# Attention weights of heads 0 to 7 transposed on TensorE instead of VectorE and DMA, with the feed-forward weights decoded earlier

## The chip, the cores and the metric

The kernel runs on one core of a Trainium2 chip. The metric is the device time of one execution in microseconds (us). Three runs of the kernel before took 759.37, 759.25 and 757.38 us; the median is 759.25 us. Engines are named as in the profile: PE (TensorE matmuls), PEld (its weight loads), DVE (VectorE), ACT (ScalarE), POOL (GpSimd), SP (the queue that issues the DMAs).

## The reference, cut to what matters

Two layers over 8 batches of 576 tokens; all numbers are float32.

```python
# attention: 64 heads (8 batches x 8 heads), 576 tokens, head dimension 64
scores = q @ k.T / 8;  cum = cumsum(max(s, 0))
scores = where(causal, -1e9, scores + min(-(cum[i] - cum[j]), 0))
attn   = softmax(scores);  x = attn @ v          # heads side by side: 576 x 512 per batch
# feed-forward with a gate over the sequence
h = gelu(x @ w_in); u, v = h[:, :512], h[:, 512:]
v = layernorm(v) * g_ln
out = x + (u * (w_sg @ v + b_sg)) @ w_out
```

## The kernel before, in words

Heads run in pairs; batch b is heads 8b to 8b+7, and its feed-forward part starts when its fourth pair is done, beside the attention of batch b+1. Thus heads 0 to 7 have no feed-forward work beside them. What fills that stage otherwise is the preparation of the feed-forward weights: `w_in` and `w_out` arrive as 64-bit floats (tile `wraw`, 16 and 8 pieces) and are decoded by integer operations (tiles `wbits`, `wm`) into a high and a low part (`wi`, `wo`); `w_sg` (`wst`, `ws`) is only split in two.

One head is five strips of scores, 64, 192, 320, 448 and 576 columns wide (1600 in all). Heads 0 to 11 (`NQ = 12`) use plain float32 matmuls on a prepared tile `kf`; later heads load `raw` and split it into `k` and `low`. Each strip goes through `softmax` (line 912): PE writes scores into PSUM (`sc`, the widest strip `sx`), DVE adds the mask and finds the row extreme `mn`, ACT takes the exponential in place and sums it (`sum`), and DVE's STREAM_TRANSPOSE turns it into the SBUF tile `ex`. That instruction transposes 32x32 blocks, so quarters of 32 partitions of a 64x64 block end up in the wrong place.

`shuffle` (line 970) mends this once per pair: two DMAs copy quarters of `ex` to a side tile `pt`, two DMAs move other quarters inside `ex`, and then ACT and POOL each copy 32x1600 numbers from `pt` back to `ex`. Only then can `pv` (line 990), PE's product of the weights with `v` into the tiles `xx`, start. It is recorded as one group, and DVE then scales `xx` into `xr` by the row `rb`, which has come from `sum` by way of two small DMAs (`rd`, `rb`). `ex` has room for two pairs. PSUM holds six one-bank tiles (tag `m`, shared by `sc`, `xx` and the feed-forward tiles `vm`, `um`, `sm`, `om`) and one two-bank tile for `sx`.

No instruction is written in its final place. Everything is recorded with a key (a position in units of heads: `POS` at line 58, `place` and `spread` at lines 1169 to 1190), a table `SHIFT` (line 74) moves kinds of operations by some units, and `plan` (line 549) lists all operations engine by engine, choosing the next by key among those that are ready by its own estimates. The order of each engine, SP's included, is then fixed in the program. Because all instructions are emitted by one helper, the profile gives them all line L528; they are told apart by their tiles.

Of the kernel before, what the change touches and what calls it, by code (L numbers as in the profile page):

```python
# [49 lines left out]
NQ = 12  # L50
U2 = 5
# [6 lines left out]
POS = dict(load=-2.0, split=-1.0, sc=(0, 0, 0, 0), sh=0.0, pv=1.9, wv=(0.1, 7.5),  # L58
           wu=(7.0, 10.0), ws=(9.0, 11.0), wo=(11.0, 14.0), f0=2.0, f1=9.6)
# [34 lines left out]
    "act copy k 128x576 raw": (-8.09, 6.2, -1.34, 101.2, 0.56),
    "act copy k 64x576 raw": (5.62, 5.49, 15.59, 99.03, 9.86),
    "act copy low 64x576 raw": (12.89, 12.94, 12.94, 0.06, -5.16),
    "act copy vt 64x512 vm": (-8.41, -2.47, -2.5, -5.05, -5.92),
    "act copy wi 128x256 wbits": (-0.48, 5.93, -3.16, 3.66, -17.79),
    "act copy wo 128x256 wbits": (-14.55, 8.67, 10.51, -13.27, 9.97),
    "act copy wr 128x576 wst": (0, -2.7, -2.97, -2.88, -0.18),  # L100
    "act copy wr 1x576 wst": (-12.69, -14.66, -18.24, -15.87, -18.2),
    "act copy ws 128x576 wst": (-13.38, -11.05, -21.02, -1.37, -1.37),
# [6 lines left out]
    "dve memset low 2x1152 -": (2.18, 1.59, -4.4, -13.47, 5.93),  # L109
    "dve memset maska 128x320 -": (0.83, 0.03, 3.82, 1.89, 0.62),  # L110
    "dve memset maskb 128x576 -": (-0.22, 0.2, 0.2, -0.22, -0.22),
    "dve memset sum 128x1 -": (-5.69, -7.9, -7.65, -6.26, -6.98),
    "dve memset sum 128x52 -": (-11.23, 7.01, 0.55, 0.74, 0.74),
    "dve memset vnr 33x512 -": (2.86, -3.96, 1.53, -17.46, -2.87),
# [3 lines left out]
    "dve reciprocal sum 128x10 sum": (14.09, 0.44, 0.44, 35.34, 6.22),  # L118
# [32 lines left out]
    "dve transpose rb 128x32 sum": (0.03, 0.03, 0.03, 0, -0.11),  # L151
# [1122 lines left out]
```

## Time and profile before

| | us |
|---|---|
| median of three runs | 759.25 |
| the profiled execution, its own time | 762.57 |
| its span from first to last instruction | 760.9 |
| PE busy in the span | 692.3 |
| DVE, ACT, POOL busy | 577.5, 536.8, 485.7 |

The page gives busy time by engine and, in 40 slices of 19 us each, the busy tenths of each engine and the TensorE clock that was granted, in tenths of its full speed. Other views of the same trace name, for each engine, whom it waited for and how long, list instructions in order of time, and sum the busy time of every engine in a stretch. A count such as x68 is the number of instructions; a plain float32 matmul shows as two instructions on PE.

### The profile page before, as it was taken

The numbers are of one execution on the slowest core, as the hardware profiler recorded it, in microseconds if no ns is written. First come the engines' busy times: TensorE is split into PE (matmuls) and PEld (weight loads), VectorE is DVE, ScalarE is ACT, GpSimd is POOL, SyncE is SP. The second block draws the span as 40 slices with busy tenths as digits, with TensorE's granted clock in tenths as the row PEclk, the third lists the DMA queues.
The fourth block names the chain that finished last, engine by engine and source line by source line (L and its number), as shares of the span: only waits on it lengthen the run. The fifth ranks groups of instructions, "written<-read, shape, count | busy, mean of one in ns | idle before, by whom it ended". The sixth has DMA issues, their size and how long they took to land.

```text
span 760.9 us, 16999 instructions
## 1 busy us (share of the span) xinstructions
PE 692.3 (91%) x5858; PEld 620.5 (82%) x5858; DVE 577.5 (76%) x1657; ACT 536.8 (71%) x1290; POOL 485.7 (64%) x634
## 2 busy tenths in 40 slices
PE   7567587799998999989998999989998999999998
PEld 5355376699887989889887989889987989899998
DVE  8775869987688776978688877978687877973752
ACT  4654578787779786878688886978688876952431
POOL 6242678878666866667756865767756865753631
PEclk9777888889999999999999999999999999999999
DMA  7564875525364363445444464435454464423101
GB/s 222 140 171 125 220 173 147 144 81 149 102 170 132 110 171 111 114 127 160 120 125 132 119 161 120 121 111 163 117 127 128 127 155 133 107 79 85 54 9 62
DMA packets 64974, 97.47 MB, mean 128 GB/s; under 512 B 19972, under 2 KB 44676, under 8 KB 64888
## 3 DMA queue, kind: packets, MB, share of 16 engines
q1 hardware_dynamic: 64888, 96.39, 46.9%
q8 instruction: 46, 0.75, 0.4%
q14 instruction: 40, 0.33, 0.2%
HBM read 56.72 MB, written 10.26 MB: 88 GB/s over the span
## 4 chain that ended last, share of the span: by engine, by line
PE 48%; DVE 12%; DMA 10%; ACT 9%; POOL 6%; issue 3%; SPq 0%; POOLq 0%; DVEq 0%; ACTq 0%
PE sm L528 10%; PE vm L528 9%; PE om L528 9%; PE xx L528 8%; PE um L528 7%; DMA raw<-in_kq 4%; PE sc L528 3%; DVE ex L528 3%; ACT sc L528 2%; DMA pt<-ex 2%; PE sx L528 2%; ACT k L528 2%; DVE sc L528 2%; DMA out_t<-ot 2%; DVE u L528 1%
## 5 line engine op out<-in xcount | busy, mean ns | idle before, releaser
L528 ACT ACTIVATE sc<-sc,mn 64x64 f32<-64x64 f32 (+3 forms) x256 | 112.4, 439 | 42.1 <-DVE mn L528 39.2
L528 PE MATMUL sm<-ws,vn 128*128 128x288 f32 x768 | 130.3, 307 | 0.4 <-DVE ex L528 0.2
L528 PE MATMUL um<-xs,wi 128*128 128x288 f32 x768 | 119.7, 304 | 8.0 <-DVE ex L528 5.0
L528 PE MATMUL om<-gt,wo 128*128 128x288 f32 x768 | 119.7, 298 | 2.6 <-POOL gt L528 2.2
L528 DVE STREAM_TRANSPOSE ex<-sc 64x64 f32<-64x64 f32 (+3 forms) x256 | 107.0, 430 | 17.2 <-ACT sc L528 16.0
L528 PEld LDWEIGHTS um<-xs,wi 128*128 128x128 f32 x768 | 110.0, 194 | 10.3 <-DVE ex L528 5.2
L528 PE MATMUL xx<-ex,v 64*64 64x128 f32 (+4 forms) x2176 | 100.3, 334 | 18.1 <-ACT ex L528 13.8
L528 PEld LDWEIGHTS xx<-ex,v 64*64 64x64 f32 x2176 | 87.2, 146 | 35.5 <-ACT ex L528 16.5
L528 PEld LDWEIGHTS sm<-ws,vn 128*128 128x128 f32 x768 | 113.5, 196 | 2.6 <-DVE ex L528 1.2
L528 PEld LDWEIGHTS om<-gt,wo 128*128 128x128 f32 x768 | 107.7, 188 | 6.4 <-POOL gt L528 3.2
L528 ACT CAST k<-raw 128x576 fp32r<-128x576 f32 x156 | 104.8, 672 | 10.8 <-DMA raw<-in_kq 5.7
L528 PE MATMUL vm<-wi,xs 128*128 128x512 f32 (+1 forms) x416 | 110.7, 399 | 0.6 <-POOL xs L528 0.4
L528 PEld LDWEIGHTS vm<-wi,xs 128*128 128x128 f32 (+1 forms) x416 | 74.1, 184 | 17.0 <-POOL xs L528 2.3
L528 POOL TENSOR_TENSOR k<-raw,k 64x576 fp32r<-64x576 f32 x52 | 74.0, 1423 | 9.2 <-ACT k L528 6.9
L528 POOL TENSOR_TENSOR gt<-u,gt 128x288 fp32r<-128x288 f32 x64 | 50.8, 806 | 43.6 <-ACT gt L528 43.2
L528 DVE CUSTOM_DVE_ANT_0 sc<-sc,maska 128x192 f32<-128x192 f32 (+2 forms) x192 | 66.8, 355 | 15.4 <-PE sc L528 14.2
L528 POOL TENSOR_TENSOR low<-raw,k 64x576 fp32r<-64x576 f32 x52 | 73.9, 1422 | 4.4 <-DMA wst<-in_w_sgt 1.9
L528 DVE SCALAR_TENSOR_TENSOR u<-u,um 128x288 f32<-128x288 f32 x128 | 55.7, 441 | 27.6 <-ACT u L528 21.7
L528 POOL TENSOR_SCALAR ex<-pt 32x1600 f32<-32x1600 f32 x32 | 48.9, 1529 | 39.7 <-DMA ex<-ex 30.9
L528 PE MATMUL sc<-k 128*128 128x320 f32 (+1 forms) x208 | 60.3, 300 | 6.9 <-DVE vnr L528 4.2
L528 DVE TENSOR_TENSOR xr<-xx,rb 128x320 f32<-128x320 f32 x64 | 27.0, 447 | 50.1 <-PE xx L528 50.1
L528 ACT CAST gt<-u 128x288 fp32r<-128x288 f32 x64 | 25.8, 429 | 54.0 <-DVE u L528 42.7
(101 smaller groups left out, 1424.0 us busy)
## 6 DMA issues: line engine op xcount, KB each, us to landing
v<-in_vp SPq DMA_DIRECT2D x32, 576.0 KB
raw<-in_kq SPq DMA_DIRECT2D x52, 288.0 KB
pt<-ex SPq DMA_DIRECT2D x64, 200.0 KB
ex<-ex SPq DMA_DIRECT2D x64, 200.0 KB
rb<-rd SPq DMA_DIRECT2D x64, 160.0 KB
out_t<-ot SPq DMA_DIRECT2D x64, 144.0 KB
wraw<-in_w_in SPq DMA_DIRECT2D x16, 256.0 KB
kf<-in_kf SPq DMA_DIRECT2D x11, 292.5 KB
```

Source lines behind the costliest of these rows:

```text
L528: real[i] = [getattr(op["eng"].real, name)(*[f(a) for a in args], **{k: f(v) for k, v in kw.items()}).ins for args, kw in calls]
```

## The change

For heads below `NE = 8`, ACT writes the exponential not in place but into the side tile `pt` (each strip has its own columns, `EO`). PE then transposes it in pieces of 64x64: a matmul with the piece as the stationary operand and a 64x64 identity as the moving one, whose result goes back into the same PSUM tile. ACT copies the strip from PSUM to `ex`. There are 49 such matmuls for a head (1 + 2 x (3 + 5 + 7 + 9)), recorded per strip as one group called `turn`. DVE's transposes of these heads and the whole `shuffle` of the first four pairs are gone, and `pv` of these pairs has an earlier key (0.9 instead of 1.9). The identity lies in the last 64 columns of `wo` until those are decoded. The keys of the weight preparation are moved forward (`w_in` over heads 0 to 10 instead of 0 to 17, `w_out` from 7.5 instead of 11), and all of `SHIFT` is new, so every engine's order is planned again; the planner also has a cost for `turn` and for PE after a pause.

```diff
+NE = 8
+EO = [0, 64, 256, 576, 1024]
...
-POS = dict(load=-2.0, split=-1.0, sc=(0, 0, 0, 0), sh=0.0, pv=1.9, wv=(0.1, 7.5),
-           wu=(7.0, 10.0), ws=(9.0, 11.0), wo=(11.0, 14.0), f0=2.0, f1=9.6)
+POS = dict(load=-2.0, split=-1.0, sc=(0, 0, 0, 0), sh=0.0, pv=1.9, pe=0.9, wv=(0.1, 4.0),
+           wu=(3.5, 6.0), ws=(6.0, 8.0), wo=(7.5, 9.5), f0=2.0, f1=9.6)
...
-    "dve transpose ex 128x576 sx": (-13.44, -12.28, 343.35, 317.33, 0),
+    "dve transpose ex 128x576 sx": (-8.08, 20.99, 161.81, 299.85, -1.96),
...
+    eye = wo[:, NC - 1, 1, DM - 64:DM]
+    ident = eye.bitcast(F32)
+    nc.vector.memset(ident, 0.0)
...
         c = 5 * (h % 2) + it
-        nc.scalar.activation(out=o, in_=o, func=AF.Exp, bias=mn, scale=-1.0, accum_out=sums[h // 2 % 2][0:r, c:c + 1])
         n = w // 64
-        nc.vector.transpose(out=xt_[0:r].pattern(base(h) + 32 * cell(h % 2, it, 0), (32, n), (RG, 2), (1, 32)), in_=o)
+        e = o if h >= NE else pt_[0:r, EO[it]:EO[it] + w]
+        nc.scalar.activation(out=e, in_=o, func=AF.Exp, bias=mn, scale=-1.0, accum_out=sums[h // 2 % 2][0:r, c:c + 1])
+        x = xt_[0:r].pattern(base(h) + 32 * cell(h % 2, it, 0), (32, n), (RG, 2), (1, 32))
+        if h >= NE:
+            nc.vector.transpose(out=x, in_=o)
+            return
+        calls = []
+        for j in range(n):
+            for g in range(r // 64):
+                rows, cs = slice(64 * g, 64 * g + 64), slice(c0 + 64 * j, c0 + 64 * j + 64)
+                calls.append(((pst[rows, cs], e[rows, 64 * j:64 * j + 64], ident[rows]), dict(start=True, stop=True)))
+        nc.group(calls, "turn")
+        nc.scalar.copy(out=x, in_=o)
...
         if h % 2:
-            place(h + POS["sh"], shuffle, h)
-            place(h + POS["pv"], pv, h)
+            if h >= NE:
+                place(h + POS["sh"], shuffle, h)
+            place(h + POS["pv" if h >= NE else "pe"], pv, h)
```

On PE, around the first group `xx` (the weights of heads 0 and 1 times `v`), the order before is this. `sc<-kf` and `sx<-kf` are score matmuls.

```order
L528 MATMUL sc<-kf 128x320
L528 MATMUL sc<-kf 128x192
L528 MATMUL sc<-kf 128x448
L528 MATMUL sc<-kf 128x64
L528 MATMUL sx<-kf 128x256
L528 MATMUL sx<-kf 128x320
L528 MATMUL xx<-ex,v 64x320 x2
...
L528 MATMUL xx<-ex,v 64x2x32 x8
L528 MATMUL sx<-kf 128x256
L528 MATMUL sc<-kf 128x320
```

The same place now, where `sc<-wo,pt` and `sx<-wo,pt` are the transposing matmuls (`wo` holds the identity):

```order
L546 MATMUL sc<-wo,pt 64x64 x20
L546 MATMUL sx<-wo,pt 64x64 x18
L546 MATMUL sc<-kf 128x448
L546 MATMUL sc<-kf 128x64
L546 MATMUL sc<-wo,pt 64x64 x11
L546 MATMUL sx<-kf 128x256
L546 MATMUL sx<-kf 128x320
L546 MATMUL xx<-ex,v 64x320 x2
...
L546 MATMUL xx<-ex,v 64x2x32 x8
L546 MATMUL sc<-wo,pt 64x64 x20
L546 MATMUL sx<-wo,pt 64x64 x18
```

Before, nothing but scores stands ahead of the group and behind it; now transposes of later heads stand between the scores and directly behind the group.

On SP, from the request of `kf` for a later head to the small transfers for the first pair (`rd`, `rb`), before:

```order
L528 DMA kf<-in_kf 65x1152
L528 DMA pt<-ex 32x1600 x2
L528 DMA kf<-cf 1x16x36
L528 DMA rd<-rb 128x32
L528 DMA kf<-in_kf 65x1152
L528 DMA ex<-ex 32x1600 x2
L528 DMA rb<-rd 64x4x160 x2
```

And now:

```order
L546 DMA kf<-cf 1x16x36
L546 DMA wraw<-in_w_in 128x512 x2
L546 DMA rd<-rb 128x32
L546 DMA kf<-in_kf 65x1152
L546 DMA rb<-rd 64x4x160 x2
```

The four shuffle transfers of the pair are gone, and two pieces of `w_in` stand ahead of `rd`.

On DVE, the decoding of `w_out` (`wbits<-wraw,wbits`) stood before among the steps of batch 0's feed-forward part (`vt`, `vm`, `bs`, `u`), in the rows that lead up to the sixth pair's `xr`:

```order
L528 SCALAR_TENSOR_TENSOR wbits<-wraw,wbits 128x256
L528 SCALAR_TENSOR_TENSOR vt<-vm,bs,g_b 128x512
L528 STREAM_TRANSPOSE ex<-sc 64x2x32
L528 SCALAR_TENSOR_TENSOR wbits<-wraw,wbits 128x256
L528 SCALAR_TENSOR_TENSOR vm<-vt,vm 128x512
L528 SCALAR_TENSOR_TENSOR wbits<-wraw,wbits 128x256
L528 BN_STATS bs<-vm 128x6
L528 SCALAR_TENSOR_TENSOR wbits<-wraw,wbits 128x256
```

Now the last larger run of it stands behind the fourth pair's `xr`, among the softmax steps of the next heads:

```order
L546 STREAM_TRANSPOSE ex<-sx 128x9x2x32
L546 STREAM_TRANSPOSE ex<-sc 128x3x2x32
L546 SCALAR_TENSOR_TENSOR wbits<-wraw,wbits 128x256
L546 STREAM_TRANSPOSE ex<-sc 64x2x32
L546 TENSOR_SCALAR wbits<-wbits 128x256
L546 SCALAR_TENSOR_TENSOR wbits<-wraw,wbits 128x256 x4
L546 ISA sc,mn<-sc,maska 128x320
```

Of the 16 instructions of this kind, 7 now stand ahead of the fourth pair's `xr`, 7 between it and the fifth's, and 2 behind that.

## Rows read from the trace of the kernel before

**Rows 1.** From the page: span, PE busy, and PE's granted clock in 40 slices

```profile
span 760.9 us, 16999 instructions
...
PE 692.3 (91%) x5858; PEld 620.5 (82%) x5858; DVE 577.5 (76%) x1657; ACT 536.8 (71%) x1290; POOL 485.7 (64%) x634
...
PEclk9777888889999999999999999999999999999999
```

**Rows 2.** Four stretches: busy us of each engine (instructions), clock, DMA share, GB/s

```profile
0.00:101.00 101.00, 67.91 (x436) 50.50 (x437) 71.89 (x231) 53.28 (x150) 46.14 (x57) 0.81 0.69 176
101.00:180.00 79.00, 67.38 (x543) 59.95 (x546) 70.33 (x191) 63.22 (x150) 66.02 (x85) 0.89 0.51 138
180.00:696.00 516.00, 495.46 (x4458) 451.09 (x4459) 401.71 (x1168) 399.15 (x946) 346.39 (x442) 0.98 0.47 128
696.00:761.00 65.00, 61.59 (x428) 58.99 (x427) 33.55 (x69) 21.17 (x44) 27.11 (x52) 1.00 0.13 41
```

**Rows 3.** PE's waits from 0 to 101 us: total, times, longest

```profile
PE xx L528 <- ACT ex L528: 12.3, 3, 5.5
PE sx L528 <- DVE ex L528: 8.0, 4, 3.2
PE sc L528 <- DMA kf<-cf: 4.8, 2, 4.5
PE xx L528 <- DVE ex L528: 4.3, 1, 4.3
```

**Rows 4.** The first pair's shuffle in order of time: start, us, what, idle before

```profile
24.43 1.20 SPq L528 DMA_DIRECT2D pt<-ex  x2
...
29.68 1.15 SPq L528 DMA_DIRECT2D ex<-ex  x2
...
34.60 1.52 ACT L528 COPY ex<-pt 32x1600 f32<-32x1600 f32 x1 [0.86 <-DMA ex<-ex]
...
36.18 5.92 PE L528 MATMUL xx<-ex,v 64*64 64x320 f32 x68 [2.80 <-ACT ex L528]
```

**Rows 5.** Stretches at half clock before 101 us: the first, the last and the sum of six

```profile
22.20:29.00 6.80, 5.61 (x12) 3.93 (x13) 4.41 (x19) 3.43 (x13) 0.84 (x1) 0.50 0.42 107
...
93.90:100.60 6.70, 4.85 (x66) 4.25 (x68) 1.61 (x5) 4.53 (x8) 4.37 (x5) 0.50 0.83 180
sum 36.70, PE 30.32 PEld 24.44 DVE 16.79 ACT 17.41 POOL 10.43; mean PE 5.05 PEld 4.07 DVE 2.80 ACT 2.90 POOL 1.74
```

**Rows 6.** The group xx alone, fourth and eighth pair: PE, PEld, DVE (xr), clock

```profile
95.00:101.00 6.00, 5.12 (x68) 4.38 (x68) 0.07 (x1) 0.53 0.78 177
179.00:183.00 4.00, 2.72 (x68) 2.43 (x68) 0.32 (x1) 1.00 0.28 89
```

**Rows 7.** ACT's copies out of PSUM near the start

```profile
8.38 0.58 ACT L528 COPY cf<-cps 64x512 f32<-64x512 f32 x1 [0.90 <-PE cps L528]
...
11.07 0.21 ACT L528 COPY cf<-cps 64x64 f32<-64x64 f32 x1
```

**Rows 8.** All that touches tile ex from 0 to 101 us, columns as in rows 2

```profile
0.00:101.00 101.00, 21.42 (x272) 17.83 (x272) 23.50 (x50) 6.10 (x4) 6.38 (x5) 0.81 0.69 176
```

**Rows 9.** PE's waits from 101 to 180 us

```profile
PE um L528 <- DVE ex L528: 4.8, 1, 4.8
PE sc L528 <- DVE vnr L528: 4.2, 1, 4.2
PE xx L528 <- ACT ex L528: 1.5, 1, 1.5
```

**Rows 10.** The two stretches at half clock between 101 and 180 us, summed

```profile
sum 16.60, PE 10.72 PEld 10.11 DVE 15.94 ACT 14.33 POOL 13.99; mean PE 5.36 PEld 5.05 DVE 7.97 ACT 7.16 POOL 7.00
```

**Rows 11.** DVE's decoding of w_out from 101 to 180 us: busy, mean ns

```profile
L528 DVE SCALAR_TENSOR_TENSOR wbits<-wraw,wbits 128x256 int32<-128x256 int32 x16 | 10.8, 691 | 0.0
...
L528 DVE TENSOR_SCALAR wbits<-wbits 128x256 int32<-128x256 int32 x8 | 2.6, 341 | 0.0
```

**Rows 12.** PE in order of time: the eighth pair's group

```profile
179.91 2.72 PE L528 MATMUL xx<-ex,v 64*64 64x320 f32 x68
```

More of the change, by code (lines that the diff above doesn't have):

```diff
@@ L94 @@
[L94 to L101, printed above, removed]
@@ L102 @@
-    "act copy ws 128x576 wst": (-13.38, -11.05, -21.02, -1.37, -1.37),
[6 rows of a table removed]
[L109 to L114, printed above, removed]
[3 rows of a table removed]
-    "dve reciprocal sum 128x10 sum": (14.09, 0.44, 0.44, 35.34, 6.22),
[8 rows of a table removed]
@@ L151 @@
-    "dve transpose rb 128x32 sum": (0.03, 0.03, 0.03, 0, -0.11),
[36 rows of a table removed]
-    "pool affine_select maska 128x320 maska": (20.47, 20.46, 23.3, 37.02, 17.85),
-    "pool affine_select maskb 64x576 maskb": (0.74, 0.74, 0.74, 0.84, 6.57),
-    "pool affine_select tri 128x576 tri": (0, 0.28, 0, 0, -2.22),
-    "pool memset ex 64x256 -": (90.59, 7.5, 15.91, 7.96, 2.48),
-    "pool memset tri 128x576 -": (3.23, 2.82, 2.79, 2.58, -4.95),
[3 rows of a table removed]
-    "pool tensor_scalar wbits 128x256 wbits": (-0.11, -0.11, -0.11, -0.22, -0.22),
[5 rows of a table removed]
@@ L209 @@
-    "pool tensor_tensor ws 128x576 wst": (-1.35, -2.41, -3.2, -6.37, -5.24),
[8 rows of a table removed]
-    "sp dma_start low 2x1152 cum": (-16.97, -14.24, 0, 0, 0),
[6 rows of a table removed]
-    "sp dma_start vnr 64x512 vnr": (3.8, -4.4, -0.39, 0, -2.26),
[5 rows of a table removed]
[8 rows of a table added]
+    "act activation sum 128x10 sum": (2.37, 19.59, 13.71, 10.1, -4.95),
[4 rows of a table added]
+    "act activation vnr 64x512 vm": (-20.83, -9.82, -11.06, 13.51, -4.98),
[4 rows of a table added]
+    "act activation wbits 128x256 wraw": (120.53, 16.23, 5.41, -19.69, -21.25),
+    "act copy cc 64x576 cf": (2.35, 2.54, 0, 0, 1.09),
+    "act copy cf 64x512 cps": (-14.42, -14.42, -5.6, -6.35, -5.95),
@@ new lines @@
+    "act copy cf 64x64 cps": (4.29, -0.7, 15.03, 12.37, 1.65),
[7 rows of a table added]
+    "act copy k 128x576 raw": (-24.6, -10.23, 27.43, 140.24, 10.53),
+    "act copy k 64x576 raw": (3.02, 2.43, 1.63, 1.48, 0.02),
+    "act copy low 64x576 raw": (39.01, 7.35, 19.5, 35.5, 19.95),
+    "act copy vt 64x512 vm": (6.21, 0.18, 0.59, 0.17, 7.42),
+    "act copy wi 128x256 wbits": (-44.27, -16.34, 1.18, 6, 6.06),
+    "act copy wo 128x256 wbits": (9.74, 9.79, -0.07, 9.91, 10.79),
+    "act copy wr 128x576 wst": (9.48, 9.45, 9.33, 9.33, 19.62),
@@ new lines @@
+    "act copy wr 1x576 wst": (9.95, 8.8, 3.25, 20.74, 10.99),
+    "act copy ws 128x576 wst": (-0.79, 0.09, 0.09, 0.09, -6.13),
[6 rows of a table added]
+    "dve memset low 2x1152 -": (3.97, 4.3, 0.77, 0.83, 8.28),
+    "dve memset maska 128x320 -": (-16.02, -16.02, -6.21, 1.94, -0.74),
+    "dve memset maskb 128x576 -": (-14.06, -26.54, -22.7, -16.17, 0.45),
+    "dve memset sum 128x1 -": (2.81, 2.56, 4.45, 4.2, 7.69),
+    "dve memset sum 128x52 -": (0, 1.2, 1.2, -10.66, 0),
[4 rows of a table added]
+    "dve reciprocal sum 128x10 sum": (32.73, 23.56, 42.82, 9.93, 2.98),
[8 rows of a table added]
@@ new lines @@
+    "dve scalar_tensor_tensor wbits 128x256 wraw": (492, 790.43, 21.72, 16.38, 13.62),
+    "dve scalar_tensor_tensor wm 128x256 wraw": (0, 0, -0.08, -1.5, -1.43),
+    "dve tensor_copy sp 128x320 st": (5.7, 0.05, -2.97, -5.44, -3.4),
+    "dve tensor_scalar vm 64x512 vm": (22.65, 111.57, 190.26, 3.28, 17.44),
+    "dve tensor_scalar wbits 128x256 wbits": (0.61, 140.81, 311.23, 0.1, 0),
+    "dve tensor_scalar wm 128x256 wbits": (0.39, 0.39, 0.39, -2.39, 0.91),
+    "dve tensor_tensor cf 64x512 cps": (2.29, 2.25, 5.13, 1.81, -0.08),
@@ new lines @@
+    "dve tensor_tensor cf 64x64 cps": (4.74, 4.74, 3.76, 3.76, -2.13),
[3 rows of a table added]
+    "dve tensor_tensor vnr 64x512 vm": (-6.89, -6.93, -6.93, -6.93, -7.32),
[12 rows of a table added]
+    "dve transpose rb 128x32 sum": (-11.73, -15.45, -5.7, -7.4, -8.78),
[39 rows of a table added]
+    "pool affine_select maska 128x320 maska": (3.31, 0.76, 0.76, 0.76, 0.34),
+    "pool affine_select maskb 64x576 maskb": (12.07, -14.38, -17.93, 0, 0),
+    "pool affine_select tri 128x576 tri": (-6.71, 0.49, -13.91, -24.27, -33.8),
+    "pool affine_select wo 64x64 wo": (0, -0.15, -0.74, 0, 0),
@@ new lines @@
+    "pool memset ex 64x256 -": (16.9, 3.26, -3.6, -3.64, -3.27),
+    "pool memset tri 128x576 -": (0.3, 0.84, -2.03, 2.27, 1.82),
[4 rows of a table added]
+    "pool tensor_scalar wbits 128x256 wbits": (-22.31, -19.04, 51.76, -22.67, -1.93),
[5 rows of a table added]
+    "pool tensor_tensor k 64x576 raw": (-4.96, -7.77, -0.92, -11.73, -5.72),
+    "pool tensor_tensor low 64x576 raw": (19.15, 13.01, 91.78, 0.09, 36.8),
+    "pool tensor_tensor vn 128x512 vt": (3.2, 0, 0, 0, 0),
+    "pool tensor_tensor wi 128x256 wbits": (4.24, -7.58, -13.2, -7.79, -13.12),
@@ L361, in add, with group @@
         return len(self.ops) - 1
-    def group(self, calls):
+    def group(self, calls, name="group"):
         ins = [v for args, _ in calls for v in args[1:]]
-        self.ops.append(dict(eng=self.tensor, name="group", args=calls, kw={}, ins=ins, outs=[args[0] for args, _ in calls],
+        self.ops.append(dict(eng=self.tensor, name=name, args=calls, kw={}, ins=ins, outs=[args[0] for args, _ in calls],
                              after=self.gate, key=self.key + self.late))
@@ L386, in cost @@
             if name == "group":
-                d, load = 2750.0, 54.0
+                d, load = 2800.0, 54.0
+            elif name == "turn":
+                d, load = 30.0 + 56.0 * len(op["args"]), 54.0
             else:
@@ L525, in emit @@
             f = lambda x: x.make() if isinstance(x, View) else x
-            calls = op["args"] if op["name"] == "group" else [(op["args"], op["kw"])]
-            name = "matmul" if op["name"] == "group" else op["name"]
+            many = op["name"] in ("group", "turn")
+            calls = op["args"] if many else [(op["args"], op["kw"])]
+            name = "matmul" if many else op["name"]
             real[i] = [getattr(op["eng"].real, name)(*[f(a) for a in args], **{k: f(v) for k, v in kw.items()}).ins
@@ L601, in plan @@
     start, fin = [0.0] * n, [0.0] * n
-    pest = peocc = pefree = moved = 0.0
+    pest = peocc = pefree = moved = cold = 0.0
     done = [0.0] * 5
@@ L636, in plan @@
         if e == PE:
+            if s > pest + peocc + 2700:
+                cold = s + 5500
+            if s < cold:
+                d *= 2
             waited = not port and s > pest + peocc + 25 and at[i] + load > s - 1
@@ L811, in tile_attn_gmlp @@
     ws = const.tile([P, NT, 2, S], F32R, name="ws")
+    eye = wo[:, NC - 1, 1, DM - 64:DM]
+    ident = eye.bitcast(F32)
+    nc.vector.memset(ident, 0.0)
+    for r0 in (0, 64):
+        nc.gpsimd.affine_select(out=eye[r0:r0 + 64], in_=ident[r0:r0 + 64], pattern=[[1, 64]], base=0, channel_multiplier=-1,
+                                compare_op=ALU.not_equal, fill=1.0)
     wr1 = const.tile([P, S], F32R, name="wr1")
```

33 lines of the change are left out of this document (9 added, 24 removed), and 228 rows, old and new, of the table SHIFT.

## The prediction

> **What bounds the kernel now.** I read the page first: the share of PE, then PE's clock in slices. PE is busy for 91% of the span, and it runs at full speed from the tenth or eleventh slice on, but at seven to nine tenths before [rows 1]. So the kernel has two regimes. The view of four stretches shows them: from 180 us on, PE is busy 495.5 of 516 us and then 61.6 of 65, while no other engine passes 80% [rows 2]. There only less PE work would help, and the change takes none away. Up to 101 us, where the fourth pair's group `xx` ends, PE is busy only 67.9 of 101 us at a clock of 0.81; between 101 and 180 us DVE is busy 70.3 of 79 us and PE 67.4 at 0.89 [rows 2]. What is lost there delays all that follows, since the steady part starts when it is over.
>
> Next I read whom PE waits for in the first stretch. Its idle time is 101 - 67.9 = 33.1 us. Half of it, 12.3 + 4.3 = 16.6 us, is `xx` waiting for `ex` in its four groups [rows 3]; the view in order of time shows what stands behind: the transfers to `pt` are issued at 24.43, those inside `ex` at 29.68, ACT's copy starts at 34.60, and PE starts at 36.18, nearly 12 us after the issue [rows 4]. Another 8.0 us is `sx` waiting for its PSUM tile, and 4.8 us a small transfer [rows 3].
>
> Each such pause costs twice. In six stretches, 36.7 us in all, the granted clock is 0.50, that is 1.2 instead of 2.4 GHz, and PE is busy 30.3 us in them [rows 5]; `xx` takes 5.12 us there (5.92 for the first pair [rows 4]) and 2.72 us at 1.00 [rows 6]. So about 15.2 of the 67.9 us are the price of the clock, and the work itself is 52.7 us at full speed.
>
> **The change, part by part.** I use the profiled execution (762.57 us) and set it against the median at the end.
>
> *Transposes on PE, added.* The trace has no 64x64 matmul against an identity; the nearest row is `xx`, whose matmuls have the same 64x64 stationary piece. A pair's `xx` streams 5760 columns (90 pieces of 64) spread over the four quarters of the array, 1440 for each, in 2.72 us [rows 6]. A head's transposes are 49 x 64 = 3136 columns over two quarters (rows 0 to 63 and 64 to 127), 1568 each: 2.72 x 1568 / 1440 = 2.96 us at full clock. If the two halves did not overlap it would be 5.9 us, and with the clock down 5.12 x 1568 / 1440 = 5.6 us. I take 2.96, as `xx` shows quarters at work together: 8 x 2.96 = +23.7 us of PE work. This is on the path, PE being the engine with most work in that stage afterwards.
>
> The Trainium skill (TensorEngine Tiling (Array Packing), section Restrictions and Gotchas) says that different row tiles write to different PSUM banks and cannot use the same bank at the same time. The two row halves of a transpose write one strip, in one bank, whereas in `xx` they write two tiles; no run here shows which holds. By that rule the halves go one after the other, the 5.9 us just given.
>
> *The shuffle's wait, removed.* 16.6 us of idle PE in four places [rows 3]. What is late next is ACT's copy out of PSUM, which now stands before `xx`: 0.21 us for 64 columns and 0.58 for 512 [rows 7], so 0.16 us and 0.00083 us a column, 5 x 0.16 + 1600 x 0.00083 = 2.1 us a head in five strips. The order puts the next heads' scores and transposes between a pair's last strip and its `xx`, so PE has work meanwhile. The row `rb` takes its way through DRAM as before; DVE reaches `xr` about two heads' softmax later in its queue, some 18 us when ten heads take 90, and the shuffle's larger transfers took 10 us from 24.43 to ACT's start at 34.60 [rows 4], so I count that wait at nothing. Uncovered it would hold DVE's queue, and two of six PSUM tiles with it, for up to those 10 us per pair.
>
> *Other idle time of PE.* 33.1 - 16.6 = 16.5 us is left. The 8.0 us of `sx` and the 4.8 us for `kf` can now be filled with transposes, but `sx` is also held longer (transposes and copy), so I take half of 12.8 as gained, 6.4; between 0 and 12.8. Left: 10.1 us.
>
> *Clock.* The low stretches follow pauses of PE [rows 4, 5]. With most long ones gone I keep 3 of the 15.2 us; between 0 and 23, the upper end if the transposes run low too.
>
> *Sum to the end of the fourth `xx`:* 52.7 + 23.7 + 10.1 + 3 = 89.5 us instead of 101.0, that is -11.5. At best 52.7 + 23.7 + 3.7 = 80 (-21); at worst 52.7 + 23.7 + 16.5 + 15.2 = 108 (+7), and more if the transposes cost double.
>
> *The other engines there.* DVE was busy 23.5 us on `ex` for ten heads [rows 8], 2.35 a head, and loses eight of them, 18.8 us. ACT gains 8 x 2.1 = 16.8 us of copies and loses the four copies from `pt`, 6.1 us [rows 8]; 53.3 + 10.7 and some us of earlier decoding make about 70, below PE's 76. POOL loses its copies (6.4 us with a memset [rows 8]). SP issues 16 transfers less ahead of the requests for `kf`, and DMA was 0.69 busy [rows 2]; the `w_in` and `w_out` pieces that come forward fill part of that room. None of these sets the end if PE is the fullest; I count them at nothing.
>
> *Decoding moved forward.* Between 101 and 180 us PE is idle 79 - 67.4 = 11.6 us, of which 4.8 and 4.2 are waits for a DVE that is behind [rows 9], and it runs at half clock for 10.7 us of work, so 5.4 more [rows 10]. DVE decodes `w_out` there: 16 x 691 + 8 x 341 ns, 13.4 us as the rows sum it [rows 11]. In the new order 9 of the 16 and 2 of the 8 still come behind the fourth pair's `xr`: 9 x 0.691 + 2 x 0.341 = 6.9 us. So DVE has 6.5 us less in its fullest stretch. I take -6.5; at best both gaps and the clock, 9.0 + 5.4 = -14.4; at worst 0.
>
> *From there on* the order of PE per pair is the same but for a few score matmuls; nothing, give or take 3 us.
>
> **Sum:** -11.5 - 6.5 = -18, so 744.6 us for an execution like the profiled one. That one lies 3.3 us above the median of 759.25, so I predict 741 us, 2.4% faster. A difference of about 0.3% (2.3 us) is what a measurement of this kernel can tell from none.
>
> **Rivals.**
>
> 1. *Everything fills.* The order leaves PE no long pause in either stretch: -21 and -14.4, 759 - 35 = 724 at the far end; I give it 728. For it: DVE loses 18.8 us, and PE's work is in many small pieces. Against it: exponential, transposes and copy go round three engines in each strip.
>
> 2. *The copy takes the shuffle's place.* `xx` still waits in each of its four groups, now for ACT, whose queue also holds exponentials and decoding. If half of the 16.6 us and of the clock's 12 us stay, 14 us of the 18 are lost: 755. For it: ACT gets the largest addition. Against it: the new order puts work of other heads in between.
>
> 3. *The transposes cost double (slower).* In heads 0 to 7, 5.9 us a head instead of 2.96, be it that the halves do not overlap or that the clock stays low; price 8 x 2.94 = 23.5 us, 741 + 23.5 = 765. It decides once a head's transposes take over 2.96 + 18 / 8 = 5.2 us. For it: nothing in the trace shows the halves in one bank, and this stage ran low before. Against it: `xx` overlaps four quarters, and fewer pauses mean less time at the low clock. That the halves take turns is what the restriction on row tiles in the Trainium skill (TensorEngine Tiling (Array Packing), Restrictions and Gotchas) would make of it.
>
> The Trainium skill (TensorE: Matmul & The Clock Gate, Part 4: PE-mode transpose) says that a transpose in the engine's own mode does not count as activity for the clock. These are plain matmuls, so I expect it not to apply; no row of before shows it.
>
> 4. *It doesn't do what it says.* That the wait stays because the shuffle stays is excluded: SP's new order has no `pt` transfer before the fifth pair's.
>
> **Chances.** The forecast 0.50 (its own range 734 to 749), rival 1 0.22, rival 2 0.14, rival 3 0.14. Rival 2 is faster in about two of three cases, rival 3 slower in most: faster 0.83, within 0.3% 0.06, slower 0.11. The range that should hold it 8 times in 10 is 724 to 761: it includes most of rivals 1 and 2 and leaves out rival 3.
>
> **What would show it.** Right: the fourth `xx` ends near 90 us and the eighth starts near 162 instead of 179.9 [rows 12]; PE's waits have no `xx` for `ex` in the first four groups; the clock is above 0.9 in the first 90 us; a head's 98 PE instructions of transposes cover about 3 us. Wrong: `xx` waiting for ACT's copy (rival 2); transposes of 18 in `sx` taking over 2 us instead of 2.96 x 18 / 49 = 1.1 (rival 3); no PE gaps at all before 160 us (rival 1); or a stretch from the eighth `xx` to the end that is not 761 - 180 = 581 us long within 4.

## The result, and the profile after

The changed kernel takes 728.55 us (median of 4 runs, 728.24 to 729.96); the kernel before took 759.31 us beside it (4 runs). The ratio is 0.960, with a 95% interval of 0.957 to 0.963. The forecast was 741 us; the time lies in the range, 12.5 us below the likeliest value.

From the page of the changed kernel, the lines that answer to [rows 1]: span, busy time, and the granted clock in 40 slices.

```profile
span 728.2 us, 18515 instructions
...
PE 692.0 (95%) x6642; PEld 622.5 (85%) x6642; DVE 558.2 (77%) x1618; ACT 540.3 (74%) x1326; POOL 481.4 (66%) x632
...
PEclk9999999999999999999999999999999999999999
```

PE is busy as long as before, although it has 784 instructions more: what the transposes add, the clock gives back. The digit of the clock is 9 in every slice, where [rows 1] had seven to nine in the first ten.

The four stretches, cut at the same places in the work as [rows 2] (end of the fourth pair's `xx`, start of the eighth's, the last part):

```profile
0.00:88.22 88.22, 78.32 (x1207) 60.48 (x1207) 58.39 (x191) 60.71 (x188) 51.87 (x66) 1.00 0.61 175
88.22:165.26 77.04, 68.19 (x560) 58.66 (x560) 68.94 (x201) 64.18 (x157) 58.92 (x76) 1.00 0.51 135
165.26:668.00 502.74, 488.61 (x4480) 448.81 (x4481) 399.43 (x1162) 396.00 (x942) 346.43 (x443) 1.00 0.48 132
668.00:728.20 60.20, 56.85 (x398) 54.60 (x396) 31.47 (x65) 19.45 (x42) 24.14 (x49) 1.00 0.13 39
```

The first stretch is 12.7 us shorter (100.9 to 88.2), the second 2.0 (79.0 to 77.0), and everything from the start of the eighth pair's `xx` on 18.0 (580.9 to 563.0). The last figure is the surprise: the forecast had nothing there, give or take 3 us, and had named a length other than 581 us within 4 as a sign of being wrong.

PE's waits from 0 to 88.2 us, which answer to [rows 3]:

```profile
PE xx L546 <- DVE wbits L546: 2.7, 2, 1.4
PE wm L546 <- DVE wz L546: 2.1, 1, 2.1
PE cps L546 <- DVE sp L546: 2.0, 1, 2.0
PE sc L546 <- DMA kf<-cf: 1.2, 1, 1.2
```

No group `xx` waits for `ex`; the 16.6 us of [rows 3] are gone, and so are the 8.0 us of `sx`. (The step `wbits` that is named for 2.7 us touches no tile of `xx`; what the group waited for there stays open. It was not ACT's copies: the last ones ahead of these two waits, of 1.4 and 1.3 us, had ended 2.1 and 1.4 us before the waits did.)

PE in order of time: 96 of the 98 transposing instructions of one head, and the fourth and the eighth pair's groups (start, us, what, idle before):

```profile
18.05 0.56 PE L546 MATMUL sc<-wo,pt 64*64 64x64 f32 x12
18.45 1.22 PE L546 MATMUL sx<-wo,pt 64*64 64x64 f32 x36
19.50 1.57 PE L546 MATMUL sc<-wo,pt 64*64 64x64 f32 x48
...
85.49 2.72 PE L546 MATMUL xx<-ex,v 64*64 64x320 f32 x68
...
165.26 2.72 PE L546 MATMUL xx<-ex,v 64*64 64x320 f32 x68 [0.89 <-ACT ex L546]
```

The 18 transposes of `sx` (36 instructions) cover 1.22 us, near the 1.1 forecast and far from the 2.2 (twice that) of halves that take turns. The fourth group takes 2.72 us where [rows 6] had 5.12, since the clock is up. All transposes together (PE's busy time on tile `wo`, same stretch):

```profile
0.00:88.22 88.22, 28.01 (x784) 1.00 0.61 175
```

Where do the 18.0 us behind the eighth pair come from? The steady part repeats in batches of four pairs. One batch of each kernel, from the 12th pair's `xx` to the 16th's, columns as in [rows 2]; before:

```profile
267.70:352.74 85.04, 81.55 (x730) 74.50 (x729) 67.36 (x197) 67.15 (x161) 58.41 (x75) 0.98 0.47 130
```

and after:

```profile
247.63:329.66 82.03, 79.83 (x730) 73.15 (x729) 66.91 (x199) 67.23 (x160) 58.61 (x75) 1.00 0.48 136
```

The same 730 matmul instructions take 3.0 us less: 1.7 us are busy time at another clock, 1.3 are pauses (3.5 to 2.2). The place is one per batch. Before, PE in order of time:

```profile
238.63 3.45 PE L528 MATMUL um<-xs,wi 128*128 128x288 f32 x24 [0.23 <-DVE u L528]
244.17 0.55 PE L528 MATMUL sx<-k 128*128 128x256 f32 x1 [2.09 <-DVE ex L528]
```

The stretch that follows there, as a window with the columns of [rows 2]:

```profile
244.06:247.47 3.41, 3.30 (x14) 3.33 (x15) 1.71 (x4) 3.18 (x5) 2.37 (x2) 0.50 0.49 133
```

and the same place after:

```profile
219.69 1.86 PE L546 MATMUL um<-xs,wi 128*128 128x288 f32 x12 [0.23 <-DVE u L546]
222.16 1.84 PE L546 MATMUL um<-xs,wi 128*128 128x288 f32 x12 [0.61 <-DVE u L546]
225.02 0.36 PE L546 MATMUL sx<-k 128*128 128x256 f32 x1 [1.01 <-DVE ex L546]
...
225.72 1.19 PE L546 MATMUL sm<-ws,vn 128*128 128x288 f32 x7
```

PE waits for the one tile `sx`, which DVE's transposes free. Before, the wait is 2.09 us in one piece, and the clock is 0.50 for the next 3.41 us (at 244, 329, 414, 500 and 585 us). After, some score matmuls stand between the `sx` matmuls of the head before (not shown), `um` pauses by itself, the wait is 1.01 us, and the clock stays at 1.00. 3.30 us of work at half clock is 1.65 us lost; with the shorter pauses that is the 3.0 us of a batch.

### The profile page after: what moved, and what is told of

Read it like the earlier page. It is cut to its first block, busy times and chain, and to the rows that moved or that the text cites. A ratio compares the mean times of both kernels' runs of the same rounds, so it can differ in the third digit from the quotient of the medians.

```text
span 728.2 us, 18515 instructions
## 1 busy us (share of the span) xinstructions
PE 692.0 (95%) x6642; PEld 622.5 (85%) x6642; DVE 558.2 (77%) x1618; ACT 540.3 (74%) x1326; POOL 481.4 (66%) x632
## 4 chain that ended last, share of the span: by engine, by line
PE 66%; DVE 16%; DMA 6%; ACT 5%; POOL 3%; issue 2%; SPq 1%; DVEq 0%; POOLq 0%; ACTq 0%
PE sm L546 14%; PE om L546 13%; PE vm L546 10%; PE xx L546 10%; PE sc L546 8%; PE um L546 7%; PE sx L546 4%; DVE ex L546 3%; DVE sc L546 3%; DMA pt<-ex 2%; DVE vm L546 2%; DVE sx L546 2%; DVE u L546 1%; DMA ex<-ex 1%; DMA rb<-rd 1%
## 5 line engine op out<-in xcount | busy, mean ns | idle before, releaser
L546 PE MATMUL sm<-ws,vn 128*128 128x288 f32 x768 | 124.7, 298 | 0.0
L546 PEld LDWEIGHTS sm<-ws,vn 128*128 128x128 f32 x768 | 109.1, 188 | 2.7 <-DVE ex L546 0.9
L546 ACT ACTIVATE sc<-sc,mn 128x320 f32<-128x320 f32 (+1 forms) x224 | 98.1, 438 | 17.4 <-DVE mn L546 15.5
L546 DVE STREAM_TRANSPOSE ex<-sc 128x320 f32<-128x320 f32 (+1 forms) x224 | 92.7, 428 | 9.4 <-ACT sc L546 8.5
L546 PE MATMUL xx<-ex,v 64*64 64x192 f32 (+4 forms) x2176 | 89.7, 308 | 6.8 <-ACT ex L546 3.5
L546 PEld LDWEIGHTS xx<-ex,v 64*64 64x64 f32 x2176 | 78.4, 133 | 20.6 <-ACT ex L546 4.5
L546 DVE CUSTOM_DVE_ANT_0 sc<-sc,maska 128x320 f32<-128x320 f32 (+2 forms) x192 | 66.2, 352 | 28.2 <-PE sc L546 22.5
L546 PE MATMUL sc<-k 128*128 128x320 f32 x208 | 59.2, 292 | 0.4 <-DVE ex L546 0.3
L546 ACT COPY ex<-pt 32x1600 f32<-32x1600 f32 x28 | 42.8, 1528 | 14.9 <-DMA ex<-ex 14.2
L546 POOL TENSOR_SCALAR ex<-pt 32x1600 f32<-32x1600 f32 x28 | 42.7, 1525 | 13.6 <-DMA ex<-ex 11.1
```

The lines of the kernel that those rows point to most:

```text
L546: real[i] = [getattr(op["eng"].real, name)(*[f(a) for a in args], **{k: f(v) for k, v in kw.items()}).ins for args, kw in calls]
```

## The experiments

All times of the kernel before that stand beside these runs are medians of 759 to 762 us; so I compare ratios to it, the changed kernel's being 0.960. In the traces I use three marks: the start of the 12th pair's `xx`, the stretch from there to the 32nd pair's (before 425.4 us, changed kernel 410.0), and from the 12th to the end (493.2 and 480.6).

### Is it the order of the steady part?

The order is a list for each engine, so it can be put in from outside. `AT` holds the planned start times of the other kernel for all steps of head 16 and later:

```
...
+    when = [float(next(at)) if op["key"] >= 16.0 else start[n] for n, op in enumerate(nc.ops)]
+    _, start, _, seqs = plan(cost, pre, new, uses, order, bufs, [(w, n) for n, w in enumerate(when)], after)
+    when = [w if op["key"] >= 24.0 else x for w, x, op in zip(when, start, nc.ops)]
+    seqs = [sorted(s, key=when.__getitem__) for s in seqs]
```

> The changed kernel, but from the steps of head 16 on the instructions of every engine follow the order of the kernel before (word for word from head 24 on, with some mixing between); the start, with its transposes on TensorE and its early decoding, is that of the changed kernel. Theory A (the 18 us behind the eighth pair come from the new order of the steady part, a PE gap of 1.0 instead of 2.1 us per batch and no 3.4 us at half clock behind it): between the 12th and the 32nd pair's group xx it takes 425 us as before (changed kernel: 410), the half-clock stretch is back once per batch, and the time is 741 to 746 us. Theory B (the changed start leaves the engines in a better phase, and the order of the steady part does not matter): 728 to 730 us, 410 us between these groups.

> The opposite: the start of the kernel before (shuffles in all pairs, decoding as before), but from the steps of head 16 on the order of the changed kernel (word for word from head 24 on). Theory A: 410 us between the 12th and the 32nd pair's group xx, clock at 1.00 there, 741 to 747 us. Theory B: 425 us there and 757 to 761 us.

The changed start with the old steady order: 748.77 us, ratio 0.982 (0.978 to 0.986). The old start with the new order: 755.66 us, ratio 0.992 (0.990 to 0.995). From the 12th to the 32nd pair's `xx`, the first of these kernels:

```profile
258.08:684.14 426.06, 409.08 (x3652) 372.93 (x3651) 333.19 (x966) 327.41 (x779) 284.10 (x364) 0.98 0.48 129
```

and the second:

```profile
272.29:680.67 408.38, 397.47 (x3638) 365.46 (x3637) 330.74 (x965) 326.37 (x776) 278.26 (x358) 1.00 0.49 134
```

So this stretch follows the order and not the start, on both sides and to within 2 us: theory A holds, B is out. In the old order a half-clock stretch is back in each batch; in the new there is none. Both totals miss what A gave (741 to 746 and 741 to 747): they lie 3 and 9 us above it. Most of that stands between the eighth and the 12th pair, where the two orders are mixed: that took 93.4 us with the old start (87.8 before), with a half-clock stretch of 6.8 us in it, and 89.4 with the changed start (82.4 in the changed kernel), whose eighth `xx` also came 3.4 us later.

### Is it the pause or the clock?

In the kernel before, two DVE instructions moved in each of five batches:

```
+        if (ks[d[p]], ks[d[p + 1]]) == ("dve scalar_tensor_tensor vm 64x512 vm", "dve tensor_tensor_reduce sx 128x576 sx"):
+            d[p], d[p + 1] = d[p + 1], d[p]
+            ...
+            d.insert(r + 1, d.pop(q))    # transposes of sx behind those of sc 128x448
```

> The kernel before with two DVE instructions moved in each of five batches: the reduction of sx goes ahead of the 0.75 us step vm<-vm,bs,g_b, and the transposes of sx ahead of those of the 320 columns of sc. Nothing else changes. The PE gap of 2.09 us should shrink to about 1.3. Theory C (the half-clock stretch follows the length of that gap): the stretches go too, 5 x (0.8 + 1.7) = 12.5 us, 747 us. Rival D (the clock falls there for another reason, as the work around it): they stay, 5 x 0.8 = 4 us, 755 us.

761.2 us, ratio 0.999 (0.996 to 1.001): no gain at all. PE at that place in order of time:

```profile
325.54 0.36 PE L528 MATMUL sx<-k 128*128 128x256 f32 x1 [1.28 <-DVE ex L528]
...
327.10 1.82 PE L528 MATMUL sm<-ws,vn 128*128 128x288 f32 x7 [0.78 <-DVE ex L528]
```

and the window behind it:

```profile
327.39:330.81 3.42, 3.42 (x20) 2.95 (x23) 0.64 (x1) 3.31 (x4) 2.76 (x2) 0.50 0.43 106
```

The pause was not taken away but cut in two: 1.28 us for `sx` and 0.78 us for the tile of `sm`, which DVE also frees and which has become late. With 2.06 us of pauses in 2.8 us the clock falls as with 2.09 in one piece. My expectation C priced only the first of them.

So I shortened the pause by work that nobody needs. In the kernel before, the first matmul of a group `um` is issued nine times:

```
+        if ks[p[i]] == "pe matmul sx 128x256 k" and all(ks[j] == "pe matmul um 128x288 wi" for j in p[i - 24:i]):
+            nc.ops[p[i - 12]]["again"] = 8
...
+            calls = [(op["args"], dict(start=True, stop=True))] * op.get("again", 0) + calls
```

> The kernel before with work added that nobody uses: in five batches the first matmul of the second um group ahead of the long pause is issued nine times instead of once, 8 x 0.13 = 1.07 us more of PE work per batch. The pause of 2.09 us should shrink to about 1.0, the tile sx being ready at the same time as before. Theory C2 (the clock falls after about 2 us of pauses close together and not after 1 us): no half-clock stretch follows, 5 x 1.7 = 8.5 us less than before, ratio 0.989, though more work is done. Rival D (the clock falls for another reason, or the added work pushes the pause ahead of it): the same time as before or up to 5 us more, ratio 1.00 to 1.007.

753.95 us, ratio 0.990 (0.986 to 0.994). PE at that place in order of time:

```profile
320.47 4.49 PE L529 MATMUL um<-xs,wi 128*128 128x288 f32 x32 [0.32 <-DVE u L529]
326.01 0.36 PE L529 MATMUL sx<-k 128*128 128x256 f32 x1 [1.05 <-DVE ex L529]
```

and the window from the 12th to the 32nd pair's `xx`:

```profile
264.70:684.10 419.40, 406.83 (x3685) 372.11 (x3684) 332.19 (x966) 327.64 (x779) 284.39 (x365) 1.00 0.48 130
```

More work, the same tile at the same time, and the kernel is 1% faster: the pause is 1.05 us, the clock stays at 1.00, the stretch takes 419.4 instead of 425.4 us. That isolates the clock's part: the time and the clock are those of C2, and D is out. (What C2 says of the length of a pause is not a rule: see the last section.) Of the 15.4 us that the changed kernel gains between these marks, 6.0 are the clock's (four of the stretches lie there, 4 x 1.65 = 6.6); the rest is shorter pauses, and 14 matmul instructions that stand behind the 32nd group instead of ahead of it.

### Can the rest of the pause go?

In the changed kernel the same idea on DVE and ACT, and, as another kernel, on PE alone:

```
+            d[p + 1:p + 5] = [s320, sx, u2, s448]                              # DVE: reduction of sx earlier
+            d.insert(p + 5, d.pop(at(DVE, p, "dve transpose ex 128x576 sx")))  # and its transposes
+            a.insert(r, a.pop(q))                                              # ACT: its exponential
...
+            p[i:i + 4 + n] = p[i + 4:i + 4 + n] + p[i:i + 4]                   # other kernel, PE: sm x7 ahead of sx x4
```

> The changed kernel with the same idea in five batches: on DVE the reduction of sx goes ahead of u and of the 448 columns of sc, the transposes of sx directly behind these; on ACT the exponential of sx ahead of that of the 448 columns. The PE gap of 1.01 us there should fall to about 0.1. If PE is what bounds the steady part: 5 x 0.9 = 4.5 us less, 724 us. Rival: the moved steps make PE late at another place (u, or the tiles of sc, which come free later): 728 us or more.

> The changed kernel with the four sx matmuls that end the pause of 1.0 us placed behind the seven sm matmuls that follow them, in five batches (PE's order alone changes). The tile for sm was free 0.8 us before the pause began. If nothing else is late: the pause goes, xx then waits for ACT's copy, which ends 0.7 us before xx now starts, so 5 x 0.6 = 3 us less, 725.5 us, ratio to before 0.9555. Rival: another pause opens at once, behind sx or ahead of xx, and the time stays at 728 to 729, ratio 0.960.

732.42 us, ratio 0.962 (0.959 to 0.965), and 732.86 us, ratio 0.964 (0.961 to 0.968): neither is better than the changed kernel. The place in the first,

```profile
305.69 0.28 PE L546 MATMUL sx<-k 128*128 128x256 f32 x1
...
307.71 1.20 PE L546 MATMUL sm<-ws,vn 128*128 128x288 f32 x7 [1.32 <-DVE ex L546]
```

and in the second:

```profile
304.16 1.85 PE L546 MATMUL um<-xs,wi 128*128 128x288 f32 x12 [0.61 <-DVE u L546]
307.71 1.20 PE L546 MATMUL sm<-ws,vn 128*128 128x288 f32 x7 [1.70 <-DVE ex L546]
308.75 0.28 PE L546 MATMUL sx<-k 128*128 128x256 f32 x1
```

`sm` starts at 307.71 in both, and in the changed kernel a batch later than 225.72, at 307.74. So `sm` waits for its tile, whatever stands ahead of it. My statement that the tile was free 0.8 us before the pause was wrong: I had taken the transposes of the 320 columns for its release. The time fits those of the last strips, as DVE has them in the changed kernel:

```profile
224.10 0.77 DVE L546 STREAM_TRANSPOSE ex<-sx 128x576 f32<-128x576 f32 x1
224.81 0.71 DVE L546 TENSOR_SCALAR vm<-vm,bs 64x512 f32<-64x512 f32 x1
225.44 0.49 DVE L546 STREAM_TRANSPOSE ex<-sc 64x64 f32<-64x64 f32 x2
```

The first of these two strips ends just ahead of `sm` at 225.72, behind a step of `vm`; in the two kernels above the same pair of strips starts at 307.42 and 307.43, 0.3 us ahead of `sm`. A version that moves them ahead of `vm` as well was not tried.

### What do the two parts of the start do by themselves?

Three kernels change one constant of the changed kernel, one the places of the decoding; in all of them the order from the tenth pair on is again the changed kernel's, so what differs is the start.

```
-           wu=(3.5, 6.0), ws=(6.0, 8.0), wo=(7.5, 9.5), ...      # e7, with wv=(0.1, 7.5)
+           wu=(7.0, 10.0), ws=(9.0, 11.0), wo=(11.0, 14.0), ...
-NE = 8
+NE = 0      # e9; e12: 4; e11: 12
```

> The changed kernel with the decoding of the feed-forward weights back at its old places (w_in until head 10, the gating weights until 11, w_out from head 11 to 14); the transposes on TensorE stay. By the prediction's term for the decoding: the eighth pair's xx 6.5 us later, 735 us, ratio to before 0.968. Rival (in the stretch behind the fourth pair DVE was not what the end waited for, as the changed kernel gained only 2.0 us there): 728 to 731 us, ratio 0.960, the first stretch being shorter by what the second loses.

> The changed kernel with its constant for the heads transposed on TensorE at 0 instead of 8: all pairs go through the shuffle again, the early decoding and the new keys stay, and from the tenth pair on the order of every engine is the changed kernel's. Theory P (the transposes give the 12.7 us that the first stretch gained): the fourth xx ends near 101 as before, and 741 to 744 us, ratio to before 0.975. Rival Q (undoing the early decoding cost 23 us in an earlier run, so the early decoding carries the start and the transposes little): 731 to 735 us, ratio 0.962. Rival R (each is worth little without the other): 750 us or more, ratio 0.987.

> The changed kernel with 4 heads transposed on TensorE instead of 8; from the tenth pair on the order is the same. 10 us of transposes go, two shuffles come back, each with 4.2 us of waiting and some 3 us of low clock as before: 5 us more at most, 728 to 735 us, ratio 0.960 to 0.966. Rival (the shuffles of pairs three and four wait behind requests for weights in SP's queue): 740 us or more, ratio above 0.972.

> The changed kernel with 12 heads transposed on TensorE instead of 8; from the tenth pair on the order is the same. If TensorE is full by then, 4 x 2.5 = 10 us more, less 3.5 us of xx waiting for the shuffle there: 735 to 738 us, ratio to before 0.967. Rival (the pauses between the fifth and the eighth pair take the transposes in): 728 to 731 us or less, ratio 0.960.

In the kernel with 12 heads the last heads' strips are multiplied by a part of `w_out` and not by the identity, which lies in the last 64 columns of `wo` and is overwritten by then; the instructions are the same, the results are not.

| heads on TensorE, decoding | 12th `xx` starts | from there to the end | ratio to before (95%) |
|---|---|---|---|
| 0, late (before) | 267.7 | 493.2 | 1 |
| 0, early (e9) | 266.7 | 479.2 | 0.986 (0.983 to 0.990) |
| 4, early (e12) | 261.4 | 479.8 | 0.979 (0.975 to 0.983) |
| 8, early (changed) | 247.6 | 480.6 | 0.960 (0.957 to 0.963) |
| 12, early (e11) | 262.0 | 482.5 | 0.979 (0.974 to 0.983) |
| 8, late (e7) | 272.8 | 479.7 | 0.992 (0.988 to 0.996) |

The expectations missed in most of these: e7 came 19 us above its forecast and 23 above its rival; e9 came near rival R, that each part is worth little without the other; e12 has the time of its rival, though `xx`, which late shuffles would hold up, waits for `ex` only 2.6 us in its first four groups; e11 came 6 us above the higher of its two figures. The column to the end says once more that the order gives its 13 us whatever the start. The column of the 12th `xx` says that the two parts of the start don't add up: early decoding alone gains 1.0 us, transposes alone lose 5.1, both together gain 20.1. At the eighth `xx`, ahead of the new order, it is the same: 179.9 us before, 180.0 in e9, 185.6 in e7, 165.3 in the changed kernel. (The table of keys came with both parts together; an order made for one of them alone might do better.)

Why the transposes alone lose is seen in the kernel with late decoding. Its fourth `xx` starts at 81.25 us, earlier than the changed kernel's 85.49; then PE stands still:

```profile
102.94 3.22 PE L546 MATMUL sc<-kf 128*128 128x448 f32 x6 [8.25 <-DMA kf<-cf]
...
116.28 2.26 PE L546 MATMUL sx<-kf 128*128 128x256 f32 x4 [6.80 <-issue]
```

and runs at half clock in four stretches between 97 and 165 us, which as windows sum to 27.3 us:

```profile
sum 27.29, PE 17.49; mean PE 4.37
```

The second of these pauses ends 0.1 us behind DVE's transposes of `sx`. Of the 6.3 us between DVE's reduction of `sx` and these transposes, 2.6 are four steps of decoding; DVE in order of time:

```profile
109.15 0.75 DVE L546 CUSTOM_DVE_ANT_0 sx<-sx,maskb 128x576 f32<-128x576 f32 x1
...
109.83 2.63 DVE L546 SCALAR_TENSOR_TENSOR wbits<-wraw,wbits 128x256 int32<-128x256 int32 x4
...
115.42 0.76 DVE L546 STREAM_TRANSPOSE ex<-sx 128x576 f32<-128x576 f32 x1
```

The first is a wait for the small row `kf<-cf`, whose request SP issues at 101.06. SP's one queue also holds the requests for weights, and from 84 to 118 us it stands before a request until DVE has decoded what is in the buffer:

```profile
SPq L546 <- DVE wbits L546: 8.8, 5, 4.7
```

Of these 8.8 us, 2.1 (90.1 to 92.2 us) stand right ahead of a request of `kf<-in_kf`, but the 4.7 come at 107.5, behind this pause; so the queue explains a part of it at most. That the time that the first stretch gains is given back in the second, which now has the whole decoding in less time, fits both places; no run tests it apart. Without transposes, the other way round, the first stretch is as before; PE's waits up to 180 us in that kernel:

```profile
PE xx L546 <- ACT ex L546: 13.6, 4, 6.9
PE sc L546 <- DMA kf<-cf: 11.9, 5, 6.3
```

### What does a transpose cost?

```
+            calls = calls * (2 if op["name"] == "turn" else 1)       # e6
...
-        for j in range(n):
-            for g in range(r // 64):
+        for g in range(r // 64):                                     # e10
+            for j in range(n):
```

> The changed kernel with every transposing matmul of heads 0 to 7 issued twice (the second time with the same result). Theory (the transposes lie on the path, as the sum of the prediction has them): 8 x 3.0 = 24 us or more, 752 to 758 us, ratio to before 0.99. Rival (TensorE still has some 20 us of pauses up to the eighth pair and other engines set the pace of the start): the second set fills pauses, 5 to 12 us, 733 to 741 us, ratio 0.97.

> The changed kernel; in each strip all transposes of the upper 64 rows are issued before those of the lower 64, instead of in turn. Instructions, tiles and everything else are the same. Theory (the halves overlap only because neighbouring instructions use different rows of the array): nine transposes of one half take 9 x 0.12 us and then nine of the other, 2.2 us instead of 1.2 us for sx, some 2.5 us more a head, 8 x 2.5 = 20 us as for the transposes issued twice, ratio to before 0.987. Rival (they overlap in any order, or the halves did not overlap before): no change, ratio 0.960.

Issued twice: 751.11 us, just under the 752 to 758 of the theory, ratio 0.987 (0.983 to 0.990), that is 0.0267 x 759 = 20 us more than the changed kernel for 50.7 - 28.0 = 22.7 us more of PE's time: the transposes lie on the path, as the sum had it. The strip `sx` of one head, where the changed kernel has 36 instructions in 1.22 us:

```profile
19.52 2.27 PE L547 MATMUL sx<-wo,pt 64*64 64x64 f32 x72
```

So 36 instructions more take 1.05 us more, 29 ns each, and the second set of all costs 22.7 / 8 = 2.84 us a head. One half after the other: 737.06 us, ratio 0.970 (0.967 to 0.973), 8 us more, between the 20 of the theory and the nothing of the rival; PE's busy time on `wo` in that kernel:

```profile
0.00:97.40 97.40, 40.80 (x784) 1.00 0.56 158
```

The same 784 instructions take 40.8 us instead of 28.0. So the halves do overlap, in one bank, when neighbouring instructions use different rows. The ratio of these sums is 1.5, but the rate doubles, as the starts of single instructions in the traces show: in the changed kernel two instructions of different halves start, as a rule, 7 ns apart or less, and the next two 58 to 59 ns behind them; in this kernel, within a half, each starts 58 to 59 ns behind the last. The sums differ by less because each run also has its start and its end (one instruction lasts 218 ns), and because here, too, halves overlap where one half's run meets the other's. Halves that take turns throughout would be 98 x 58 ns = 5.7 us a head by this estimate, near the 5.9 of rival 3.

## Why the prediction was right, and where it was wrong

The time lies in the range, and in the first stretch the mechanism is the one forecast. But the two stretches that the sum was about gave only 14.7 us of its 18, and the other 18.0 us were not forecast at all. That the time still lies in the range is owed to the range's width, and is luck. The changed start with the old order (e1) takes 748.77 us.

- *The shuffle's wait, removed; idle time; clock.* Right. 16.6 us of waits are gone; PE's idle time up to the fourth `xx` is 88.2 - 78.3 = 9.9 us, forecast 10.1. For the clock I kept 3 us; it is 1.00 from 5 us on, so 0.
- *Transposes on PE.* 28.0 us of busy time instead of 23.7, or 3.5 a head. The columns cost what was forecast: a second set adds 22.7 us (e6), 2.84 a head against 2.96. The other 5.3 us are the starts and ends of the short runs (36 instructions take 1.22 us, 12 take 0.56), which the scaling from `xx` left out; in part the next work runs in them already. The copies of ACT take 0.19 to 0.65 us a strip as estimated from [rows 7]. Other work is 50.3 us instead of 52.7. The term came to -12.7 instead of -11.5. The halves overlap in one bank (e10), so they did not take turns, as they would by the rule of the Trainium skill (TensorEngine Tiling (Array Packing), Restrictions and Gotchas) that row tiles can't use one bank at the same time; the measurement decides, for halves that write different partitions of the bank, as these do.
- *Decoding moved forward.* -2.0 us between the fourth and the eighth pair instead of -6.5. Idle time fell by 2.8 us (11.6 to 8.85) and the 5.4 us of half clock are gone, but 17 matmuls more stand in this stretch (560 against 543 in [rows 2]), and PE's work at full clock is 68.2 instead of 67.4 - 5.4 = 62.0 us: 6.2 us came over, from both sides, among it nine `vm` matmul instructions that stood ahead of the fourth `xx` before. Both stretches together gave 14.7 us, forecast 18.
- The form of this term failed, too. I priced the decoding by DVE's 6.5 us alone and added it to the transposes' gain. e7 and e9 show that the gain of each hangs on the other: with the transposes, the early decoding is worth 25 us at the 12th `xx`, without them 1. I had not asked what the second stretch would do if the first ended earlier with the decoding still to come.
- *"From there on ... nothing, give or take 3 us".* This is the step that failed: -18.0 us. By the stretches above and in [rows 2], 11.6 us of it are busy time and 6.4 pauses. The five half-clock stretches are 5 x 1.65 = 8.3 of the busy time; the other 3 are work that now stands ahead of the eighth pair. From the 12th pair on, 12.5 us are from the new order (e1, e2, and the table). The 5.4 us between the eighth and the 12th pair take both, the order and the start: with the new order and other starts (e7, e9) it is 87.2 and 86.7 us (before 87.8, changed kernel 82.4), without a half-clock stretch but with 82.9 and 83.8 us of PE's work there instead of 80.2; with the changed start and the old order (e1) it is 89.4. I read that the order of PE per pair was the same but for a few score matmuls, and took the steady part's 0.98 for the clock in [rows 2] as full; I did not look at the pause of 2.09 us in each batch and at the half-clock stretch behind it. The new order shortened just that pause; whether by those few matmuls or by DVE's order no run shows apart, since e1 and e2 put in the orders of all engines at once. e5 shows the clock's share.
- *Rivals.* "Everything fills" gave 728 and was 0.5 us off, but by another way: the start gained 14.7 us of its 35, and what follows the eighth pair 18.0. Of "The copy takes the shuffle's place" there is nothing in the first four groups: no wait of `xx` for ACT's copies stands in the list. "The transposes cost double" is refuted by the 1.22 us and by e10, in which a part of that price is paid.
- With the transposes as plain matmuls the clock stays at 1.00; that the engine's own mode would not (the Trainium skill, TensorE: Matmul & The Clock Gate, Part 4: PE-mode transpose) no run here shows.

## What to carry to other kernels

A steady part at 0.98 of the clock is worth a look: in a kernel that repeats, one pause of 2 us per round that costs 1.7 us more at half clock is 2% of the time, and a change made for the start can move it by accident. When a stage is shortened, ask what the next one must finish in the shorter time; two edits that are each worth nothing can be worth 20 us together, as here. And a pause for a tile is only gone when the next tile that the same engine frees is not the later one.

## What the runs showed of the hardware

Added matmuls with an unused result made the kernel 1% faster (e5), as they kept the clock up. What makes the clock fall is not settled by the length of a pause:

| pauses of PE close together, us | where | clock behind it |
|---|---|---|
| 2.09, 2.10 | before, e1 | 0.50 for 3.4 us |
| 1.28 and 0.78 | e3 | 0.50 for 3.4 us |
| 0.61 and 1.70 | e8 | 1.00 |
| 0.75 and 1.32 | e4 | 1.00 |
| 1.05, 1.01 | e5, changed kernel | 1.00 |
| 1.65 | e11 at 146.7 us | 0.50 for 3.4 us |
| 2.16 | changed kernel at 120.1 us | 1.00 |
| 2.54 | before, at 45.4 us | 1.00 for 5.0 us |

The places that are not shown above, PE in order of time, in e4, e11, the changed kernel and before:

```profile
303.99 1.86 PE L546 MATMUL um<-xs,wi 128*128 128x288 f32 x12 [0.75 <-DVE u L546]
...
148.35 2.85 PE L546 MATMUL um<-xs,wi 128*128 128x288 f32 x12 [1.65 <-DVE u L546]
...
122.27 1.95 PE L546 MATMUL xx<-ex,v 64*64 64x320 f32 x34 [2.16 <-ACT ex L546]
...
47.89 0.67 PE L528 MATMUL sx<-kf 128*128 128x256 f32 x2 [2.54 <-DVE ex L528]
```

The last three rows of the table stand against a bound on the length alone: a shorter pause is followed by half clock, two longer ones are not. Around the pause of 2.16 us, PE had none over 0.5 us from 107 us to that one, and the next comes at 128.2 us. What tells these rows from the first stays open.

Two row halves of the array that write different partitions of one bank overlap fully: two instructions of different halves start 7 ns apart or less, as a rule, and each such pair takes the 58 to 59 ns that one instruction takes within a half. In busy time of the same 784 instructions that is 28.0 against 40.8 us, as starts and ends of the runs are counted in both.
